# Loading q and k in 1 KB runs and turning them with smaller TensorE operations, in a sliding-window attention and channel-mix kernel

## The chip, the cores and the metric

The kernel runs on one core of a Trainium2 chip. The metric is the device time of one execution in microseconds (us), the median of the runs. With one core there are no dies to compare. The time before was 234.99 us, the median of 3 runs (234.88 to 235.05). Only runs in the fast state are compared. Their mean granted clock (the TensorE clock that the throttle let through, as a share of full speed) was 0.991 or more over a run.

## The reference

The first half is causal attention in a window of 128 positions with a distance bias per head. The second half is a channel mix with a shift by one position. Batch 8, 8 heads, 576 positions, 64 columns a head.

```python
def _attn_ref(q, k, v):                      # [8, 8, 576, 64], float32
    scores = scale * np.matmul(q, k.transpose(0, 1, 3, 2))
    rel = pos[:, None] - pos[None, :]
    bias = slopes[:, None, None] * (-np.abs(rel))[None, :, :]
    mask = (rel >= 0) & (rel < 128)
    scores = np.where(mask, scores + bias[None], -1e9)
    # ... softmax over the last axis ...
    return np.matmul(attn, v)

def _moe_ref(x, mu_k, mu_r, w_k, w_v, w_r):  # x [8, 576, 512], heads joined
    xk = mu_k * x + (1.0 - mu_k) * x_prev    # x_prev: one position earlier
    xr = mu_r * x + (1.0 - mu_r) * x_prev
    k = np.maximum(xk @ w_k, 0.0)            # 512 -> 1024
    v = k * k @ w_v                          # 1024 -> 512
    return sigmoid(xr @ w_r) * v             # the "receptance"
```

## The kernel before

The program is a list of operations with durations, dependencies and buffers. A list scheduler, run while the program is built, puts them in one fixed order for each engine. Each engine then works through its order and waits where data or a buffer is missing. So an edit of a duration or a priority moves instructions everywhere.

TensorE needs q and k turned, with the head's 64 columns on the partitions. They come in by several paths. The tails are the last 64 of the 576 positions.

```python
    WIDE = (1,)             # batches whose q and k are loaded head-major
    WAIT = 2.0              # how long 64-row operations may be put off
    QM = 0                  # 0: full transposes; 1: half-array ones
    XTT = range(6, B)       # batches whose tails a DMA turns
    NWARM = 90              # matmuls of a constant that keep TensorE busy early
    A = {PE: 14.25, ACT: 4.00, DVE: 4.50, VIR: 0}   # lead of attention over the mix
    NBIAS = 4               # head pairs that take the distance bias by matmul
    def SQ(order):          # engines allowed for the squares of the mix
        return (DVE,)
    # ...
    def run_load(dst, i, b, c0, r, h0, h1, deps=()):     # head-major: 64*r-value runs
        hs = (q, k)[i][b, h0:h1, c0:c0 + 128 * r].rearrange("h (p r) d -> p h (r d)", p=128)
        # ... one DMA on the software queue; r = 4 gives runs of 1 KB
    def full_load(b, i, h, g):                           # four loads in runs of 256 B
        src = (q, k)[i][b, :, 0:SM].rearrange("h (p r) d -> p h r d", p=128)
        # ...
    def tail_load(b):                                    # 64 partitions, runs of 256 B
        for i in range(2):
            src = (q, k)[i][b, :, SM:S].rearrange("h p d -> p h d")
            # ... dma_start(out=ts_buf[h.idx][64 * i:64 * i + 64], in_=src)
```

The transposes of a head pair, and the warm-up matmuls that the scheduler puts wherever its plan has TensorE idle:

```python
    for i in range(NWARM):      # lowest priority; no data, no result used
        plan.add(PE, 0.118 if i < 40 else 0.056, 0.0, [n_warm, g_wm], (1e12, i), emit_warm, ...)

    def qk_quad(b, g, nr, buf, ...):          # head-major: 32 transposes of 64x64
        for n in range(2 * nr):
            for hl, r in ((0, 0), (1, 1), (1, 0), (0, 1)):
                rows = slice(64 * r, 64 * r + 64)
                nc.tensor.transpose(
                    one(hp[r]).bitcast(BF16)[64 * hl:64 * hl + 64, 64 * n:64 * n + 64],
                    buf()[rows, n // nr, 2 * g + hl, n % nr], ident[rows, rows])
        # ... two copies of 512 columns to SBUF, on ScalarE after batch 0

    def qk_full(b, g, prio):                  # 8 transposes of 128x128
        for n in range(2 * NF):
            nc.tensor.transpose(..., cb_buf[hc.idx][:, n // NF, n % NF, 2 * g:2 * g + 2]..., ident)
        # ... one copy of 1024 columns on ScalarE

    def tails(b, prio):                       # 4 transposes of 128x128, one copy on VectorE
        for g in range(G):
            nc.tensor.transpose(..., ts_buf[hs.idx][:, 2 * g:2 * g + 2]..., ident)

    def square(e, out, in_):                  # k * k of the channel mix
        if e == ACT: nc.scalar.activation(out=out, in_=in_, func=AF.Square)
        else:        nc.vector.tensor_tensor(out=out, in0=in_, in1=in_, op=ALU.mult)
```

The softmax here doesn't subtract the row's maximum and nothing guards it: scores larger than these inputs give would overflow.

## Time and profile before

| | before |
|---|---|
| time, span of the profiled run | 234.99 us, 233.1 us |
| TensorE, VectorE, ScalarE busy | 97%, 81%, 69% |
| first receptance matmul (end of the start stage) | 37.38 us |
| last receptance group to the end of the span | TensorE dense, then a fixed end of 3.7 us |

The prediction below shows the page and the chain of waits. Here is the other view: the busy time of each engine in three stretches of 10 us. The columns are the stretch and its length, then for TensorE, its weight loads, VectorE, ScalarE and GpSimd the busy us with the number of instructions, and last the granted clock, the DMA share and GB/s.

```profile
30.00:40.00 10.00, 9.01 (x144) 6.54 (x144) 7.96 (x20) 9.47 (x19) 5.78 (x7) 1.00 1.59 181
40.00:50.00 10.00, 10.00 (x114) 5.34 (x113) 9.78 (x18) 5.85 (x9) 8.31 (x11) 1.00 2.14 176
50.00:60.00 10.00, 9.79 (x106) 6.26 (x105) 7.70 (x16) 9.30 (x17) 7.93 (x10) 1.00 2.27 186
```

### The profile page before, as it was taken

To read this page: it belongs to the slowest core of one execution; us is meant where nothing else is said; L and a number is where in the kernel's file an instruction comes from. 1 tells how busy PE (TensorE), PEld (TensorE's weight loads), DVE (VectorE), ACT (ScalarE), POOL (GpSimd) and SP (SyncE) were. 2 spreads that over 40 slices of the span, in tenths; PEclk is the share of its full clock that TensorE was granted. 3 is DMA by queue.
4 is the path that set the end of the run, shared out by engine and by line. 5 is a ranking of instruction groups with operands and counts; after the bars stand their busy time and mean duration, and the time that the engine had idled before them with its cause. 6 is when DMAs were issued, how large, how long until landed. Compare 5 with 4: busy or idle time off the path is not lost.

```text
span 233.1 us, 6268 instructions
## 1 busy us (share of the span) xinstructions
PE 225.8 (97%) x2487; PEld 135.7 (58%) x2487; DVE 189.8 (81%) x427; ACT 160.8 (69%) x292; POOL 97.7 (42%) x124
## 2 busy tenths in 40 slices
PE   7899989999999999999999999999999999999994
PEld 6576765556566765555555755455655844455462
DVE  7587988987797989989989979985769996974242
ACT  3669999759999986984984975947584726326251
POOL 8966773898883893069508935200000000000000
PEclk9999999999999999999999999999999999999999
DMA  7999999999999999989999999993232124121122
GB/s 168 178 167 196 161 162 185 153 199 201 155 154 173 109 138 207 106 106 169 201 188 100 172 181 211 155 146 106 69 89 93 45 48 146 46 90 48 65 70 90
DMA packets 131100, 31.73 MB, mean 136 GB/s; under 512 B 120056, under 2 KB 127232, under 8 KB 131072
## 3 DMA queue, kind: packets, MB, share of 16 engines
q0 software_dynamic: 102736, 16.26, 102.7%
q1 hardware_dynamic: 26592, 14.50, 26.9%
q10 hardware_dynamic: 1744, 0.59, 1.0%
q8 instruction: 19, 0.31, 0.5%
q14 instruction: 9, 0.07, 0.1%
HBM read 33.56 MB, written 9.44 MB: 184 GB/s over the span
## 4 chain that ended last, share of the span: by engine, by line
PE 84%; ACT 5%; DMA 3%; POOL 3%; issue 2%; DVE 1%; DVEq 0%; POOLq 0%; ACTq 0%
PE uno L941 27%; PE uno L907 26%; PE uno L925 14%; PE duo L716 6%; PE duo L658 5%; DMA ts<-in_k_dram 3%; PE uno L771 2%; PE uno L1154 2%; ACT at L672 2%; POOL qx L434 1%; ACT mask L1088 1%; ACT qk L628 1%; PE uno L856 1%; POOL vs L438 1%; ACT rl L914 1%
## 5 line engine op out<-in xcount | busy, mean ns | idle before, releaser
L941 PE MATMUL uno<-wv_sb,kk 128*128 128x512 bf16 (+2 forms) x296 | 71.8, 374 | 0.0
L907 PE MATMUL uno<-xk,wk_sb 128*128 128x256 bf16 (+2 forms) x416 | 69.5, 314 | 0.7 <-ACT rl L914 0.4
L672 ACT ACTIVATE at<-duo 128x1024 bf16<-128x1024 f32 (+2 forms) x68 | 65.7, 1002 | 5.4 <-PE duo L658 5.4
L914 ACT ACTIVATE rl<-uno 128x256 bf16<-128x256 f32 (+2 forms) x104 | 47.3, 492 | 20.3 <-PE uno L907 19.0
L907 PEld LDWEIGHTS <-wk_sb 128*128 128x128 bf16 x416 | 38.7, 98 | 22.1 <-issue 0.9
L685 DVE TENSOR_TENSOR at<-at,mask 128x1024 bf16<-128x1024 bf16 x56 | 37.7, 680 | 8.2 <-ACT at L672 7.8
L438 POOL DMA_DIRECT2D vs<-in_v_dram x32 | 28.4, 895 | 33.9 <-PE duo L716 30.3
L941 PEld LDWEIGHTS <-kk 128*128 128x128 bf16 x296 | 26.4, 98 | 26.2
L880 DVE TENSOR_TENSOR kk<-rl 128x256 bf16<-128x256 bf16 (+2 forms) x104 | 32.8, 334 | 9.0 <-ACT rl L914 7.8
L932 ACT ACTIVATE rs<-uno 128x512 bf16<-128x512 f32 x36 | 22.1, 614 | 26.1 <-PE uno L925 23.1
L925 PE MATMUL uno<-wr_sb,xr 128*128 128x512 bf16 x144 | 37.0, 379 | 0.5 <-ACT rl L914 0.5
L946 DVE SCALAR_TENSOR_TENSOR ot<-rs,uno 128x512 f32<-128x512 bf16 (+2 forms) x37 | 24.6, 668 | 12.1 <-PE uno L941 9.7
L716 PEld LDWEIGHTS <-at 128*128 128x128 bf16 x576 | 21.8, 98 | 6.0 <-issue 0.9
L821 DVE SCALAR_TENSOR_TENSOR xk<-dl,mu_sb,xt 128x576 bf16<-128x576 bf16 (+1 forms) x32 | 24.8, 780 | 0.4
L821 DVE SCALAR_TENSOR_TENSOR xr<-dl,mu_sb,xt 128x576 bf16<-128x576 bf16 (+1 forms) x32 | 24.4, 769 | 0.0
L463 POOL DMA_DIRECT2D cb<-in_k_dram x24 | 21.3, 901 | 7.1 <-DMA wv_sb<-in_moe_w_v_dram 3.3
L628 ACT COPY xt<-uno 128x256 bf16<-128x256 bf16 (+1 forms) x48 | 17.1, 405 | 9.0 <-PE uno L771 8.8
L925 PEld LDWEIGHTS <-xr 128*128 128x128 bf16 x144 | 13.5, 98 | 14.6 <-issue 0.7
L463 POOL DMA_DIRECT2D cb<-in_q_dram x24 | 21.2, 915 | 1.4 <-DMA vs<-in_v_dram 1.2
L628 ACT COPY qk<-uno 128x1024 bf16<-128x1024 bf16 (+2 forms) x26 | 18.8, 777 | 2.4 <-PE uno L1049 0.8
L716 PE MATMUL duo<-vs,at 128*128 128x65 bf16 x448 | 19.1, 193 | 0.0
L814 DVE TENSOR_TENSOR dl<-xt 128x576 bf16<-128x576 bf16 (+1 forms) x32 | 13.7, 434 | 4.2 <-ACT xt L628 4.2
(78 smaller groups left out, 206.8 us busy)
## 6 DMA issues: line engine op xcount, KB each, us to landing
out_dram<-ot SPq DMA_DIRECT2D x30, 256.0 KB, 5.2
vs<-in_v_dram POOLq DMA_DIRECT2D x32, 128.0 KB, 6.6
cb<-in_q_dram POOLq DMA_DIRECT2D x24, 128.0 KB, 7.0
cb<-in_k_dram POOLq DMA_DIRECT2D x24, 128.0 KB, 6.8
out_dram<-ot SPq DMA_DIRECT2D x10, 128.0 KB, 1.8
wk_sb<-in_moe_w_k_dram POOLq DMA_DIRECT2D x2, 512.0 KB, 8.8
wv_sb<-in_moe_w_v_dram POOLq DMA_DIRECT2D x2, 512.0 KB, 10.8
qx<-in_k_dram ACTq DMA_DIRECT2D x4, 128.0 KB, 4.5
```

Source lines behind the costliest of these rows:

```text
L438: return dma(POOL, 256, issue_t(1024), lambda e: nc.gpsimd.dma_start(out=vs_buf[h.idx][:, j, :, 0:D], in_=v[b, :, 128 * j:128 * j + 128].r ...
L463: return [dma(POOL, 256, issue_t(1024), lambda e, r=r: nc.gpsimd.dma_start(out=cb_buf[h.idx][:, i, r], in_=src[:, :, r]), [g]) for r in ra ...
L628: (nc.scalar.copy if e == ACT else nc.vector.tensor_copy)(out=out, in_=in_)
L672: lambda e, ah=ah, w=w, hp=hp: nc.scalar.activation(out=ah(), in_=two(hp)[:, :, 0:w], func=AF.Exp, scale=float(scale)), (), [hp])
L685: nc.vector.tensor_tensor(out=a, in0=a, in1=m, op=ALU.mult)
L716: nc.tensor.matmul(a[:, hl, t - t0], lhsT=at[:, lo:lo + 128], rhs=vs[:, u, 2 * g + hl, :] if u < NF else tvb[:, 2 * g + hl], start=(u == u ...
L821: lambda e: nc.vector.scalar_tensor_tensor(out=buf[hk.idx][:, g, e0 + c0:e0 + c1], in0=dls(), scalar=mu[:, g:g + 1], in1=xc(1), op0=ALU.mu ...
L880: nc.vector.tensor_tensor(out=out, in0=in_, in1=in_, op=ALU.mult)
L907: nc.tensor.matmul(one(hp)[:, 0:n], lhsT=wk_sb[:, po, 128 * fo:128 * fo + 128], rhs=xk_buf[hx.idx][:, po, c0:c1], start=(po == 0), stop=(p ...
L914: a = op(ACT, act_t(n), [s], pr, lambda e, hp=hp, hr=hr: nc.scalar.activation(out=rl_buf[hr.idx][:, 0:n], in_=one(hp)[:, 0:n], func=AF.Rel ...
L925: nc.tensor.matmul(one(hp), lhsT=xr_buf[hx.idx][:, po, 128 * c:128 * c + 128], rhs=wr_sb[:, po], start=(po == 0), stop=(po == NPO - 1))
L941: nc.tensor.matmul(one(hv)[:, a:b], lhsT=kk_buf[hk.idx][:, fo, o:o + 128], rhs=wv_sb[:, fo, a:b], start=(fo == 0), stop=(fo == NFO - 1))
```

## The change

The intent is to make q and k cheaper to bring in. Batches 2 and 3 are also loaded head-major in runs of 1 KB, and turned by 64x64 transposes, as batch 1 already was. The tails of batches 0 and 1 come as 1 KB runs over 128 partitions, and are turned by 16 matmuls with the identity instead of four transposes. Batch 4 goes from full to half-array transposes. The settings of the scheduler were searched again for it, so the order of all instructions differs. Squares of the first groups of the channel mix may also go to ScalarE.

```diff
-    WIDE = (1,)
+    WIDE = (1, 2, 3)
+    TW = (0, 1)
-    QUAD = 0.0565
+    QUAD = 0.040
-    WAIT = 2.0
-    QM = 0
+    WAIT = 5.0
+    QM = 1
     def SQ(order):
-        return (DVE,)
+        return (DVE, ACT) if order < 3 else (DVE,)
-    XTT = range(6, B)
+    XTT = range(5, B)
-    A = {PE: 14.25, ACT: 4.00, DVE: 4.50, VIR: 0}
-    NBIAS = 4
-    XRL = 3.0
+    A = {PE: 9.50, ACT: 6.00, DVE: 5.00, VIR: 0}
+    NBIAS = 5
+    XRL = 1.5
-    SLOPE = 4.5
+    SLOPE = 4.6
 # (the assumed DMA rates of run_load change too)
 # tail_load
+        if b in TW:
+            for i in range(2):
+                ns.append(dma(POOL, 104, issue_t(128), lambda e, i=i: nc.gpsimd.dma_start(
+                    out=ts_buf[h.idx].rearrange("p h d -> p (h d)")[:, 256 * i:256 * i + 256],
+                    in_=(q, k)[i][b, :, SM:S].rearrange("h (c r) d -> h c (r d)", r=4)), [g]))
+            return h, ns
 # tails, for b in TW
+            for n in range(8):
+                for hl in range(2):
+                    nc.tensor.matmul(
+                        one(hp)[64 * hl:64 * hl + 64, 64 * n:64 * n + 64],
+                        lhsT=ts_buf[hs.idx][:, n],
+                        rhs=ident.rearrange("p (g t c) -> p t g c", g=G, t=2)[:, hl],
+                        start=True, stop=True)
+        # two copies of 256 columns on VectorE in place of one of 512
 # (the old form stays as tails_full for the other batches; cut)
```

More of the change, by code (lines that the diff above doesn't have):

```diff
@@ L220 @@
     RATE = 284.0
-    WIDE = (1,)
+    WIDE = (1, 2, 3)
     PART_WIDE = True
-    QUAD = 0.0565
-    RUN = {2: 64 * 284 / 329.0, NF: 128 * 284 / 357.0}
+    TW = (0, 1)
+    QUAD = 0.040
+    RUN = {2: 64 * 284 / 345.0, NF: 128 * 284 / 390.0}
     FLIP = 1.25
     NO = 5
-    WAIT = 2.0
-    QM = 0
+    WAIT = 5.0
+    QM = 1
     OM = 1
@@ L843, in out_flip, with tails_full @@
         return res
-    def tails(b, prio):
-        htt = Hold("tt")
-        hs = th[b]
-        if b in XTT:
-            plan.follow(last["tt"], ttg[b])
-            last["tt"] = ttg[b]
-            return tth[b], ttl[b]
+    def tails_full(b, prio, htt, hs):
         hp = Hold("p1")
@@ L866, in tails, with emit @@
         c = [op(DVE, dve_t(512), [t, g], prio + (0,), emit_c, (), [hp])]
+        return htt, c
+    def tails(b, prio):
+        htt = Hold("tt")
+        hs = th[b]
+        if b in XTT:
+            plan.follow(last["tt"], ttg[b])
+            last["tt"] = ttg[b]
+            return tth[b], ttl[b]
+        if b not in TW:
+            return tails_full(b, prio, htt, hs)
+        hp = Hold("p1")
+        def emit(e):
+            for n in range(8):
[5 more added lines that the diff above has]
+                        start=True, stop=True)
+        t = op(PE, 0.03 * 16, list(tl[b]) + [n_ident], prio + (0,), emit, [hp], [hs])
+        g = virtual("tt", [htt])
+        c = [op(DVE, dve_t(256), [t, g], prio + (0,), lambda e, i=i: copy_any(
+            e, tt_buf[htt.idx][:, :, i].rearrange("p g (c r) -> p g c r", r=4),
+            one(hp)[:, 256 * i:256 * i + 256].rearrange("p (r g c) -> p g c r", r=4, g=G)),
+                (), [hp]) for i in range(2)]
         return htt, c
```

## The prediction

> **What bounds the kernel now.** I read the page first (busy shares, slices), then the chain of waits in order of time, then the timelines of TensorE and ScalarE over the first 60 us, and last the groups by form and the DMA queues by stretch.
>
> The page and the chain of waits:
>
> ```profile
> PE 225.8 (97%) x2487; PEld 135.7 (58%) x2487; DVE 189.8 (81%) x427; ACT 160.8 (69%) x292; POOL 97.7 (42%) x124
> ...
> PE 84%; ACT 5%; DMA 3%; POOL 3%; issue 2%; DVE 1%; DVEq 0%; POOLq 0%; ACTq 0%
> ```
>
> TensorE sets the end: 97% busy and 84% of the chain. But the busy share flatters it: before 26 us it holds 90 warm-up matmuls that compute nothing (L619), and the modelled tails of short matmuls cover gaps. So I split the span where the chain stops leaving TensorE.
>
> ```profile
> 8.60 8.04 DMA ts<-in_k_dram
> ...
> 18.08 1.30 ACT at L672 x2
> ...
> 25.84 1.56 PE uno L907 x12
> ...
> 37.38 1.02 PE uno L925 x4
> 38.41 0.55 PE duo L716 x18
> ...
> 44.43 0.55 PE duo L658 x12
> 44.98 0.97 PE uno L925 x4
> 45.95 0.86 PE uno L941 x4
> ...
> 53.23 1.02 ACT qk L628
> ...
> 85.47 0.42 ACT xt L628
> ...
> 227.23 2.18 PE uno L941 x12
> ```
>
> The reader is to see three stages. Up to 37.4 us the chain goes through a tail load of batch 0 (8 us) and then mostly through ScalarE; this is the only stage with slack. From 37.38 to 229.4 us it is TensorE alone but for two waits, 1.08 us at 53.2 and 0.46 us at 85.5. From 229.4 on there is a fixed end of 3.7 us (last eviction, store).
>
> The same chain gives prices. Four 512-column matmuls take 0.86 us (0.2155 each), 0.97 right after a group that used 64 rows of the array: a change of tiling costs about 0.11. Twelve score matmuls take 0.55, of which 0.11 is the change before them.
>
> The timeline of TensorE:
>
> ```profile
> 16.69 0.40 PE L856 MATMUL uno<-ident,ts 128*128 128x128 bf16 x4
> ...
> 32.35 0.45 PE L1002 MATMUL uno<-ident,cb 64*64 64x64 bf16 x32
> 32.73 1.05 PE L907 MATMUL uno<-xk,wk_sb 128*128 128x256 bf16 x8
> ...
> 52.58 1.50 PE L1154 MATMUL uno<-ident,cb 128*128 128x128 bf16 x24
> ```
>
> The start of the next group is what counts: 32 quarter-array transposes (one head pair of batch 1) occupy 32.35 to 32.73, 0.38 with the change of tiling, so 0.28 without. Eight full transposes (one head pair of batches 2 to 4) take 0.45 (16 of them are 0.89 or 0.90 in the chain). Ten half-array transposes (L771) take 0.25 with the change, 0.14 without.
>
> **What the Trainium skill says.** (1) "Trainium Kernel Development and Optimization", Performance Expectations: matmul busy time is a bad measure because matmuls are pipelined. The trace agrees: 97% busy, yet only about 25 us of useful matmul work lies in the first 37.4 us (below). (2) "TensorE: Matmul & The Clock Gate", Back-to-back issue gap: N / 2.4 GHz plus 2.5 ns; for 512 columns 216 ns, and the trace has 0.86 us for four. (3) "TensorEngine Tiling (Array Packing)", Key Properties: changing the tiling mode drains TensorE. The trace shows the price, 0.97 against 0.86. (4) "DMA: Bandwidth & Descriptors", Why small descriptors are slow: a fixed overhead per packet weighs heavily at 256 B. In the queue view for 17 to 24 us (mostly the 1 KB runs of batch 1) the software queue moved 1.32 MB in 7 us, 0.189 MB/us; for 62 to 70 us (256 B runs of a later batch) 1.05 MB in 8 us, 0.131 MB/us. It agrees.
>
> **The change, part by part.** Instruction counts are from the order of the built programs, prices from above.
>
> TensorE, whole program:
> - Batches 2 and 3, eight head pairs, from 8 full transposes to 32 quarter ones: 8 x (0.28 - 0.45) = -1.4 us.
> - Batch 4, four pairs, from 8 full to 16 half ones: 16 x 0.0145 = 0.23, so 4 x (0.23 - 0.45) = -0.9 us.
> - Tails of batch 5 move to the transposing DMA: -0.2 us.
> - Tails of batches 0 and 1: four full transposes (0.22) become 16 matmuls with K = 128 and 64 output rows, 64 columns each. At an issue floor of 25 to 30 ns each that is 0.4 to 0.5: 2 x +0.2 = +0.4 us. (If both column halves overlapped it would be nil.)
> - One more head pair (batch 1, first) takes its bias by matmul: 4 more of 512 columns, +0.9 us.
> - Changes of tiling shape: I counted them in both orders, with (rows, columns) as the shape: 106 before, 120 after; 14 x 0.11 = +1.5 us. The quarter transposes have a shape of their own, so they pay on both sides.
> Sum: -1.4 - 0.9 - 0.2 + 0.4 + 0.9 + 1.5 = +0.3 us. The new transposes win nothing on TensorE that the drains do not take back.
>
> Check of this bookkeeping: with these prices all matmuls from the first receptance matmul (37.38 us) to the last sum to about 191 us; the trace has 229.4 - 37.4 = 192.0, of which 1.5 are the two named waits. So that stage is dense, and only removed work or removed waits shorten it.
>
> The two waits: at 52.6 us four head pairs of full transposes are issued in a row, take all four single-bank PSUM buffers, and each is freed only by a 1.04 us copy on ScalarE. After the change the order interleaves 32 quarter transposes with score and channel-mix groups, and the copies are two of about 0.6 us. I give back 0.8 of the 1.5 us.
>
> The start: tails of batch 0 as 128 runs of 1 KB instead of 512 of 256 B per tensor. Two loads of 64 KB at 0.131 MB/us are 1.0 us of queue, at 0.189 0.7 us: they land 0.3 to 0.6 us earlier. ScalarE then works nearly without a gap (9.72 of 10 us in 20 to 30, 9.47 in 30 to 40), so what is gained there holds only if ScalarE gets no more work before the first receptance matmul. I summed its instructions up to the first receptance activation at columns / 1200 plus 0.07 us (0.10 for squares and masks): 28.0 us before, 28.2 after. Fewer relus stand ahead of it (10 instead of 16), but six squares are new there. So about even, and the first receptance matmul needs slightly less of it. TensorE has about 1 us less to do before that point (24 against 25 us), which it then does later. Net for the start: first receptance matmul 0.8 us earlier, but 1 us more left behind it, which is already in the sum.
>
> So from the first receptance matmul on: before 190.5 dense + 1.5 waits; after 190.5 + 0.3 + 1.0 (moved behind) = 191.8 + 0.7 waits = 192.5. End: 37.4 - 0.8 + 192.5 + 3.7 = 232.8 against 233.1.
>
> DMA in the middle: q and k of each of batches 2 and 3 are 1.05 MB as written, 5.5 us of queue at 0.189 MB/us instead of 8 at 0.131. This lies under a TensorE that is already full: worth nothing directly, though buffers and orders get easier.
>
> VectorE and ScalarE: 13 squares go from VectorE (13 x 0.25 = 3.3 us) to ScalarE (about 13 x 0.33 = 4.3), two mask products (1.4 us) vanish, and twelve copies of 1.04 become 24 of about 0.55. VectorE was at 9.8 of 10 us in 40 to 50, 90 to 100 and 110 to 120, so relief there can remove small stalls; ScalarE between 38 and 60 us, where it was at 5.9 to 9.3 of 10, becomes nearly full. I count -0.5 for the first (and the retuned priorities, which were presumably searched for this order) and +0.2 for the second.
>
> Sum: -0.3 - 0.3 = -0.6, and I lean a little further, to -0.9: 234.1 us.
>
> **Rivals.**
> (a) DMA-bound start. If the loads, not ScalarE, pace the first 37 us, the 1 KB runs give more: the 8.04 us tail load stands on the chain, and the POOL timeline shows issues waiting for older DMAs (2.13 us for a weight load at 13.5). Against it: after 17.4 us ScalarE has a single gap of 0.25 us. If it holds the start shrinks by 2 to 3 us: 232.
> (b) ScalarE takes over. Squares and doubled copies sit on the engine that bounds the start and nearly fill it to 60 us. My sums give ScalarE 19.7 us and TensorE about 21.5 us of work between the first receptance activation and the first 384-column relu; with such a balance any slip stalls TensorE. It would make 236 or 237.
> (c) Drains dearer than thought. If quarter transposes and the 128x64 tail matmuls pay 0.2 a change, 14 more changes make +1.3 us over my sum: 235.5.
> (d) Hidden anyway. TensorE is full from 37 us on, everything else cancels: 235.
>
> **Range and chances.** The terms are small and of both signs; (a) and (b) set the ends. Predicted 234.1 us, 8 in 10 within 231.9 to 236.2. A gain over 2% needs 230.3 or less, 4.7 us off a start that has about 12 us of slack, most of it unavoidable loading: 0.06. A loss over 2% needs 239.7: 0.03. Within 2%: 0.91.
>
> **What would show it.** TensorE's instructions rise by about 250. The tail load of batch 0 lands before 16.3 us, and the first receptance matmul starts at 36.2 to 37. The wait at 53 us is gone or below 0.5 us. A quarter group of 32 occupies 0.28 to 0.4 us, the 16 tail matmuls 0.4 to 0.5. ScalarE is over 9 of 10 us in 40 to 60; packets under 512 B fall by about 18,400 from 120,056 (2 x 8192 of q and k, 2 x 1024 of tails). I am wrong if the first receptance matmul comes 2 us earlier or later than that, if TensorE shows waits for ScalarE between 40 and 60 us, or if the stretch behind it is not 191 to 194 us.

## More of the kernel before

The timeline of TensorE shows two waits at the transposes of the tails of batch 1:

```profile
29.53 0.27 PE L856 MATMUL uno<-ident,ts 128*128 128x128 bf16 x2 [0.17 <-ACT qk L628]
30.29 0.27 PE L856 MATMUL uno<-ident,ts 128*128 128x128 bf16 x2 [0.49 <-issue]
```

They are not waits for the load: both tails of batch 1 had landed by 28.48 us. The second is put down to "issue", that is, to nothing that the profile shows.

## The result, and the profile after

| | before | after |
|---|---|---|
| time, median of 4 runs each | 235.02 us (234.88 to 235.27) | 236.23 us (235.61 to 236.46) |
| span of the profiled run | 233.1 us | 234.4 us |
| VectorE, ScalarE busy | 81%, 69% | 80%, 71% |
| first receptance matmul | 37.38 us | 36.78 us |

The ratio is 1.0046, with a 95% interval of 1.0025 to 1.0067. Here and below, a ratio is the mean time of one kernel's fast runs over the mean of the other's fast runs of the same rounds, so it is not quite the ratio of the medians. The change is the same within 2%, and slower by about 1.1 us. I had expected 0.9 us faster.

The page of the changed kernel, in the lines for busy time, DMA packets and the chain by engine:

```profile
PE 223.1 (95%) x2703; PEld 134.7 (57%) x2735; DVE 186.8 (80%) x413; ACT 165.8 (71%) x317; POOL 89.4 (38%) x116
...
DMA packets 118062, 31.90 MB, mean 136 GB/s; under 512 B 102536, under 2 KB 114064, under 8 KB 118032
...
PE 83%; ACT 9%; DMA 2%; issue 2%; DVE 1%; SPq 1%; DVEq 0%
```

The trace lacks 32 matmul records: there are 2735 weight loads and 2703 matmuls. So the busy 223.1 us is not less work. ScalarE rises from 5% to 9% of the chain. The same three stretches show where:

```profile
30.00:40.00 10.00, 7.79 (x155) 5.21 (x156) 6.18 (x15) 9.26 (x19) 4.52 (x7) 1.00 1.36 197
40.00:50.00 10.00, 9.48 (x184) 6.61 (x184) 8.97 (x16) 9.53 (x21) 6.91 (x9) 1.00 1.84 183
50.00:60.00 10.00, 9.74 (x195) 5.72 (x195) 9.39 (x19) 9.46 (x18) 7.80 (x10) 1.00 2.00 187
```

In 40 to 50 us ScalarE went from 5.85 to 9.53 us, and TensorE from 10.00 to 9.48. The chain of waits after, in that stretch, leaves TensorE for almost 9 us:

```profile
39.57 0.88 PE uno L954 x4
...
40.96 1.02 ACT at L679
41.98 0.59 ACT xt L635 x2
...
44.90 1.85 ACT at L679 x2
46.75 0.29 ACT kk L907
...
49.23 0.48 ACT qk L635
```

The pieces on ScalarE are exponentials (at), copies of turned values (xt, qk) and squares (kk), which were never on ScalarE before. In the kernel before, the chain in the same stretch is TensorE alone.

**A ledger.** TensorE is nearly dense, so I sorted its span into work and idle time. Work is the number of instructions of each kind times a price from the trace of before: 0.2155 us for 512 columns, 0.0145 for a half-array transpose, 0.0088 for a quarter one, 0.105 for each change of tiling shape, and so on; the new tail matmuls, which are only in the trace of after, at 0.0175. Idle is the start of a receptance group less the work ahead of it. The prices can be checked where TensorE is dense: from the fifth to the seventh receptance group of after (66 to 75 us) there are 9 changes of shape, 4 of them to or from the quarter transposes, and the idle time stays at 14.3 within 0.02 us. One correction is needed. The last of the four early loads of q lands at a slightly different time in each execution. This shows as the wait for it in the timeline of TensorE, here before, and then after:

```profile
7.65 1.06 PE L1046 MATMUL uno<-id,qx 128*128 128x128 f32 x7 [0.54 <-DMA qx<-in_q_dram]
```

```profile
7.97 1.05 PE L1075 MATMUL uno<-id,qx 128*128 128x128 f32 x7 [0.85 <-DMA qx<-in_q_dram]
```

The instructions up to this point are the same in both. So I take the start of the first group of bias matmuls behind the first attention group (9.57 us before, 9.89 after) as the arrival, and subtract its delay against 9.57 from all starts of a trace. In the 12 experiments it lies between 9.63 and 10.73 us. The correction is my choice. It assumes that all later work moves along, and that is not so for a wait for another load.

| us on TensorE, corrected for the arrival | before | after | difference |
|---|---|---|---|
| work ahead of the first receptance matmul | 24.57 | 23.15 | -1.42 |
| idle ahead of it | 12.81 | 13.31 | +0.50 |
| work behind it | 191.12 | 192.53 | +1.41 |
| idle from it to the third receptance group (at 45 and 50 us) | 0.01 | 0.72 | +0.71 |
| idle from there to the fifth (at 61 and 66 us) | 0.39 | 0.29 | -0.10 |
| idle from there to the last group | 0.77 | 0.59 | -0.18 |
| sum | | | +0.92 |

The corrected spans differ by 0.99 us (233.06 and 234.05), the times by 1.1. So the loss sorts itself like this: TensorE has as much work as before (-0.01 us), and 0.93 us more idle time. Of that 0.50 lies ahead of the first receptance matmul, and 0.71 between 37 and 50 us; 0.28 is won back later.

### The profile page after: what moved, and what is told of

Its sections match the earlier page's. It is cut to its first block, busy times and chain, and to the rows that moved or that the text cites. A ratio compares the mean times of both kernels' runs of the same rounds, so it can differ in the third digit from the quotient of the medians.

```text
span 234.4 us, 6737 instructions
## 1 busy us (share of the span) xinstructions
PE 223.1 (95%) x2703; PEld 134.7 (57%) x2735; DVE 186.8 (80%) x413; ACT 165.8 (71%) x317; POOL 89.4 (38%) x116
## 4 chain that ended last, share of the span: by engine, by line
PE 83%; ACT 9%; DMA 2%; issue 2%; DVE 1%; SPq 1%; DVEq 0%
PE uno L970 26%; PE uno L936 24%; PE uno L954 13%; PE duo L723 6%; PE duo L665 6%; ACT at L679 4%; DMA qx<-in_q_dram 2%; PE uno L778 2%; ACT qk L635 2%; PE uno L1031 1%; PE uno L626 1%; PE duo L652 1%; ACT rl L943 1%; ACT kk L907 1%; PE uno L723 1%
## 5 line engine op out<-in xcount | busy, mean ns | idle before, releaser
L970 PE MATMUL uno<-wv_sb,kk 128*128 128x512 bf16 (+2 forms) x280 | 69.5, 373 | 1.6 <-issue 1.1
L692 DVE TENSOR_TENSOR at<-at,mask 128x1024 bf16<-128x1024 bf16 x54 | 36.0, 676 | 6.5 <-ACT at L679 6.4
L909 DVE TENSOR_TENSOR kk<-rl 128x256 bf16<-128x256 bf16 (+2 forms) x91 | 29.8, 343 | 11.2 <-ACT rl L943 9.8
L954 PE MATMUL uno<-wr_sb,xr 128*128 128x512 bf16 x133 | 36.3, 379 | 1.2 <-ACT qk L635 0.7
L635 ACT COPY qk<-uno 128x512 bf16<-128x512 bf16 (+1 forms) x38 | 20.5, 599 | 2.4 <-PE uno L1031 1.0
L734 DVE TENSOR_TENSOR xu<-duo,rc 128x640 bf16<-128x640 f32 x20 | 16.4, 818 | 0.3
L470 POOL DMA_DIRECT2D cb<-in_k_dram x16 | 14.3, 914 | 1.3 <-DMA vs<-in_v_dram 0.8
```

The lines of the kernel that those rows point to most:

```text
L635: (nc.scalar.copy if e == ACT else nc.vector.tensor_copy)(out=out, in_=in_)
L692: nc.vector.tensor_tensor(out=a, in0=a, in1=m, op=ALU.mult)
L954: nc.tensor.matmul(one(hp), lhsT=xr_buf[hx.idx][:, po, 128 * c:128 * c + 128], rhs=wr_sb[:, po], start=(po == 0), stop=(po == NPO - 1))
L970: nc.tensor.matmul(one(hv)[:, a:b], lhsT=kk_buf[hk.idx][:, fo, o:o + 128], rhs=wv_sb[:, fo, a:b], start=(fo == 0), stop=(fo == NFO - 1))
```

## The experiments

Unless I say that the plan was made anew, an edit is made when instructions are emitted, after the scheduler has fixed the order. Then the order of all engines stays that of the kernel it starts from, and only the named instructions differ. All kernels gave correct results. The ledger of all of them:

| run | ratio to before, 95% | work | idle, first receptance | idle, third | idle, last |
|---|---|---|---|---|---|
| before | 1 | 215.69 | 12.81 | 12.82 | 13.98 |
| after | 1.0046 (1.0025 to 1.0067) | 215.68 | 13.31 | 14.03 | 14.91 |
| e1_sq_dve | 1.0045 (1.0028 to 1.0062) | 215.68 | 13.75 | 14.13 | 15.34 |
| e2_old_tails | 1.0040 (1.0021 to 1.0059) | 215.14 | 14.36 | 15.09 | 15.85 |
| e3_full | 1.0188 (1.0153 to 1.0223) | 215.78 | 13.31 | 18.61 | 19.38 |
| e4_sq_dve_replanned | 1.0251 (1.0224 to 1.0277) | 215.37 | 12.22 | 13.01 | 20.60 |
| e5_fewer_warm | 1.0011 (0.9994 to 1.0029) | 215.68 | 13.02 | 13.74 | 14.49 |
| e7_copies_dve | 1.0029 (1.0006 to 1.0052) | 215.68 | 12.82 | 13.97 | 14.73 |
| e8_before_copies_dve | 1.0038 (1.0021 to 1.0055) | 215.69 | 13.14 | 14.01 | 15.18 |
| e9_before_fewer_warm | 0.9993 (0.9972 to 1.0013) | 215.69 | 13.04 | 13.05 | 14.21 |
| e10_both | 1.0031 (1.0009 to 1.0052) | 215.68 | 12.54 | 13.89 | 14.65 |
| e11_late_sq_dve | 1.0044 (1.0000 to 1.0089) | 215.68 | 13.03 | 13.41 | 14.97 |
| n2_search | 1.0075 (1.0046 to 1.0104) | 214.46 | 11.47 | 11.48 | 16.29 |
| n2_fw | 1.0050 (1.0010 to 1.0090) | 214.36 | 12.97 | 12.98 | 16.56 |

Work and idle time are in us, summed up to the start of the first, third and last receptance group, and corrected for the arrival. n2 has another order, so its groups stand elsewhere. They come from one trace each, the ratios from 4 to 6 runs. Where the two disagree by a few tenths, I trust neither alone.

**Are the squares on ScalarE the cost?** e1_sq_dve, from the changed kernel:

```diff
-                e, kk_buf[hk.idx][:, fo, 0:n], rl_buf[hr.idx][:, 0:n]), (), [hr]))
+                DVE, kk_buf[hk.idx][:, fo, 0:n], rl_buf[hr.idx][:, 0:n]), (), [hr]))
```

> The changed kernel in its own order, with the 13 squares that its schedule gave to ScalarE run on VectorE instead; nothing else moves. Theory A (ScalarE, loaded with squares and doubled copies, stalls TensorE between 37 and 54 us, where the idle grew by about 0.7 us): 235.3 to 235.7 us, the waits of TensorE for ScalarE between 40 and 50 us shrink. Theory B (the loss is the 14 extra changes of tiling shape and the added bias): nothing moves, 236.2. VectorE has room there (6.2 of 10 us in 30 to 40), so a loss is not expected of either.

Measured: 236.46 us (236.19 to 236.72), no gain. The theory that the squares cost the difference falls as a whole, but the ledger shows why it looked right. From the first to the third group the idle time falls from 0.72 to 0.38 us: there ScalarE was too full, and moving the squares takes away about half of the wait. It is only a net gain, because the chain of e1 runs through VectorE in that stretch, from 43.2 to 48.6 us, where that of the changed kernel runs through ScalarE:

```profile
43.63 0.60 DVE at L692
...
48.37 0.21 DVE kk L909
```

The start takes this gain back, with 0.44 us more idle time ahead of the first receptance matmul. The timeline of VectorE in e1, in a part of the start where it works almost without a gap:

```profile
28.27 0.28 DVE L909 TENSOR_TENSOR kk<-rl 128x256 bf16<-128x256 bf16 x1
28.47 0.55 DVE L734 TENSOR_TENSOR xu<-uno,rc 128x384 bf16<-128x384 f32 x1
```

Squares now stand ahead of the attention outputs (xu), which TensorE needs next. In the changed kernel the same xu starts at 27.84 us instead of 28.47, with the same arrival of 9.89 us.

e4_sq_dve_replanned asks for the same, but lets the scheduler plan anew:

```diff
-        return (DVE, ACT) if order < 3 else (DVE,)
+        return (DVE,)
```

> The same choice as in the first run (squares on VectorE only), but given to the scheduler, which then lays out the whole kernel anew with the changed kernel's other settings. Theory A alone would say 235.3 to 235.7 as in the first run. Theory D (the scheduler's layout scatters by some microseconds with any setting, and both kernels are picks from that scatter): clearly slower, 238 to 241 us, with idle of TensorE in other places.

Measured: 241.35 us (240.53 to 242.01). The work is even 0.31 us less, and the idle time 5.7 us more, nearly all of it behind the third group. About 1.7 us of that is clock: the trace has a granted clock of 0.5 from 61.17 us on, for 3.41 us. Still, a new plan with one choice changed moved the time by some 5 us, far more than the edit is worth in place. That is why the other experiments keep the order, and why the separate effect of the changed settings (A, WAIT, XRL, SLOPE) could not be measured.

e11_late_sq_dve, the last run, starts from e5_fewer_warm below and moves only the squares after the first group, which run from about 37 us on (eight of the 13 by the trace, not seven):

```diff
-                e, kk_buf[hk.idx][:, fo, 0:n], rl_buf[hr.idx][:, 0:n]), (), [hr]))
+                DVE if order else e, kk_buf[hk.idx][:, fo, 0:n], rl_buf[hr.idx][:, 0:n]), (), [hr]))
```

> The changed kernel in its own order with the first 68 warm-up matmuls only (that version: 235.81 us, ratio 1.0011), and on top only the squares of the second and later channel-mix groups (7 of the 13, those after 36 us) moved from ScalarE to VectorE in place. Theory H, each stretch has its own engine at the limit: at 24 to 28 us VectorE is the full one and ScalarE squares are right, at 37 to 50 us ScalarE is the full one and VectorE has gaps of 0.2 to 0.65 us, so these squares are better on VectorE: the idle before the third receptance group falls by 0.3 to 0.4 us, 235.4 to 235.5 us, level with the kernel before. Rival I, the rest of the idle there is set by copies and exponentials that stay on ScalarE: no change, 235.7 to 235.9. Over 236 would mean VectorE is full there as well.

Measured: 237.09 us (236.43 to 237.39), where before ran from 234.71 to 237.34 on this chip. In time it is a miss, with a wide interval (1.0000 to 1.0089). Over 236 us had been the sign that VectorE is full there as well, and the chain agrees: from 43.3 to 48.7 us it runs through VectorE, as in e1. The ledger tells more. Against e5 the start is unchanged (13.03 and 13.02), the idle time from the first to the third group falls from 0.72 to 0.38, as in e1, and then it rises by 1.12 us between the fifth and the eighth group (66 to 86 us), where e5 has 0.28. Uncorrected, this trace starts a full us late: it waited 1.33 us for that load of q, against 0.54 and 0.85 in the two lines above, after a wait of 0.41 that they do not have.

So two traces agree that moving the squares between 37 and 50 us takes 0.34 us off this wait, net of what they cost on VectorE. They also agree that the later squares (three, at 61.8 to 65.8 us) are no better there: from the fifth to the eighth group e1 takes 0.48 us longer than the changed kernel, and e11 0.84 us longer than e5.

**What are the new tails worth?** e2_old_tails keeps the changed order, with the old tail loads and transposes for batches 0 and 1:

```diff
-                    out=ts_buf[h.idx].rearrange("p h d -> p (h d)")[:, 256 * i:256 * i + 256],
-                    in_=(q, k)[i][b, :, SM:S].rearrange("h (c r) d -> h c (r d)", r=4)), [g]))
+                    out=ts_buf[h.idx][64 * i:64 * i + 64],
+                    in_=(q, k)[i][b, :, SM:S].rearrange("h p d -> p h d")), [g]))
-            for n in range(8):
-                for hl in range(2):
-                    nc.tensor.matmul(...)
+            for g in range(G):
+                nc.tensor.transpose(..., ts_buf[hs.idx][:, 2 * g:2 * g + 2]..., ident)
```

> The changed kernel in its own order, with the tails of batches 0 and 1 loaded and turned in the old way (512 runs of 256 B per tensor, four full transposes each) in the same places. Bookkeeping of TensorE work: 0.9 us less (no 128x64 shape, four changes of shape fewer, 0.22 instead of 0.48 us each). Theory B (work and drains decide): 235.3 to 235.8 us. Rival C (the start is bound by the loads): the tail lands about 0.5 us or more later, and the time rises to 236.7 or more. If both are true they cancel: 236.2.

Measured: 236.28 us (235.9 to 236.97): the parts cancel. The old form needs 0.54 us less work, because 32 matmuls become 8 transposes and four changes of shape go away. But the idle time ahead of the first receptance matmul rises by 1.05 us. The tails of batch 1 are late for this order, whose plan counted on them:

```profile
28.65 0.38 PE L883 MATMUL uno<-ident,ts 128*128 128x128 bf16 x4 [0.97 <-ACT kk L904]
```

The line names ScalarE, but the k tails of batch 1 landed at 28.52 us, just before. In the changed kernel they landed at 27.18, and this group starts at 28.11 without a wait. So the new tails are worth 0.5 us at the first receptance matmul (1.05 less 0.54). At the end it is 0.4 by the ledger and nothing by the times.

**What are the head-major loads worth?** e3_full keeps the changed order, but loads batches 2 and 3 in runs of 256 B and turns them by full transposes:

```diff
 # run_load, for b in (2, 3): four loads in place of the two halves
+            nc.gpsimd.dma_start(out=cb_buf[ch[b].idx][:, i, a], in_=(q, k)[i][b, :, a:SM:4].rearrange("h p d -> p h d"))
+            for a in range(4) if h0 == 0
 # qk_quad, for b in (2, 3): 8 transposes of 128x128 in place of 32
+                for n in range(2 * nr):
+                    nc.tensor.transpose(..., cb_buf[ch[b].idx][:, n // nr, n % nr, 2 * g:2 * g + 2]..., ident)
```

> The changed kernel in its own order, with q and k of batches 2 and 3 loaded in 256 B runs (8 loads a batch as before) and turned by 64 full transposes in place of 256 quarter ones, same copies. Bookkeeping of TensorE work: +0.1 us (0.45 instead of 0.28 us each, but fewer changes of shape). Theory B: 236.1 to 236.4 us, quarter transposes and head-major loads are worth nothing. Rival C (loads matter): the 16,384 packets of 256 B that come back slow the loads of 30 to 60 us and TensorE shows waits for batch 2; 237 us or more.

Measured: 240.05 us (238.52 to 241.16), 3.8 us slower than the changed kernel (3.3 by the ratios). The work is the same within 0.1 us: dearer transposes against 12 fewer changes of shape. Most of the time goes to the load. These are TensorE's waits (in total us, times, longest us) and then the chain:

```profile
PE uno L1032 <- DMA cb<-in_k_dram: 2.5, 4, 0.7
```

```profile
40.65 6.46 DMA cb<-in_k_dram
...
47.16 0.23 PE uno L1032
```

The first eight transposes of batch 2 take from 43.28 to 47.32 us, where 0.45 would do: 3.6 us for the load. Right behind it the granted clock halves, from 47.37 us on for 3.41 us. This is one microsecond of that stretch (the clock is the third figure from the end):

```profile
49.00:50.00 1.00, 1.00 (x4) 0.34 (x3) 0.00 (x0) 1.00 (x2) 0.98 (x2) 0.50 2.31 147
```

Four matmuls of 512 columns take 1.68 us there in place of 0.86. Half clock for 3.41 us is another 1.7 us, by my estimate. The two make up the 5.3 us of idle time between the first and the third group. The times agree: the three runs with a mean clock of 0.993 or less took 240.64 to 241.16 us, the other three 238.52 to 239.46.

The loads in runs of 256 B end at 47.1 us. The changed order wants batch 2 at 43.3, where the kernel before turned it only at 51.04. The head-major loads come in halves of four heads: in the changed kernel the first half had landed at 42.70 us and the second at 45.31. So the first heads are there 4.4 us earlier than in e3, but the whole batch only 1.8. Part of the gain is thus the split by heads and not the 1 KB runs, and no run separates the two. The runs are faster all the same: loads of batch 3 land one after another at 0.193 MB/us (as written) in the changed kernel and at 0.136 in e3, those of batch 2 at 0.171 and 0.155. But before had no wait for that load at all. The earliness is needed only by the order that was built on it, and TensorE is full at that time.

**Warm-up matmuls in the way.** The changed trace has fillers around the first tails:

```profile
16.18 0.83 PE L626 MATMUL uno<-warm 128*128 128x128 bf16 x12
16.94 0.44 PE L884 MATMUL uno<-ident,ts 128*64 128x64 bf16 x16
...
18.27 0.68 PE L626 MATMUL uno<-warm 128*128 128x128 bf16 x9
18.78 0.60 PE L936 MATMUL uno<-xk,wk_sb 128*128 128x256 bf16 x4
```

They were planned into gaps that the plan expected. They have a fixed place in TensorE's order, so work behind them can't start when its data comes early. e5_fewer_warm, from the changed kernel, and e9_before_fewer_warm, the same in the kernel before as a control, emit only the first 68 of the 90:

```diff
+        n_done.append(0)
+        if len(n_done) > 68:
+            return
         nc.tensor.matmul(one(h_wm)[:, 0:128], lhsT=warm, rhs=warm, start=True, stop=True)
```

> The changed kernel in its own order, without the last 22 of its 90 warm-up matmuls, among them nine that stand for 0.5 us right before the first channel-mix group at 18.3 us. Theory E (TensorE itself loses there, because these fillers stand in its order): 0.5 us or so faster, 235.7. Theory F (ScalarE and VectorE bound the start, TensorE's place there is slack): no change, 236.0 to 236.5, the first receptance matmul at the same time.

> The control to the run without late fillers: the kernel before in its own order, without the last 22 of its 90 warm-up matmuls. Dropping them was worth about 0.8 us to the changed kernel. In the kernel before they stand ahead of the tail of batch 0, which lands only after them (16.65 us), and at 22.6 and 23.7 us. Theory E (the fillers hide the earlier tail of the changed kernel and so are part of why the change lost): 0 to 0.3 us here, 235.1 to 235.5. Rival G (fillers cost both kernels alike): about 0.8 us faster here too, 234.7, and they explain nothing of the difference.

Measured: e5 235.81 us (235.49 to 236.21), e9 235.31 (234.63 to 235.59). Ratios of 1.0011 and 0.9993: without the fillers the changed kernel is some 0.8 us faster by the ratios (0.4 by the medians and by the ledger), and in the kernel before nothing can be seen. This is not firm. The intervals of the changed kernel and of e5 overlap, and two later runs with the same fillers left out and one more edit each, e10 and e11, stand at 1.0031 and 1.0044. The timelines fit it. In e5 the tails and the first mix now wait only for a VectorE copy:

```profile
16.43 0.44 PE L887 MATMUL uno<-ident,ts 128*64 128x64 bf16 x16 [0.24 <-DVE qk L638]
...
18.17 0.60 PE L939 MATMUL uno<-xk,wk_sb 128*128 128x256 bf16 x4 [0.35 <-DVE tt L638]
```

In e9 TensorE waits for the tail load itself. It lands at 17.35 us in this trace, and landed at 16.64 in that of before, where the fillers ended at the same moment (16.69):

```profile
17.39 0.40 PE L859 MATMUL uno<-ident,ts 128*128 128x128 bf16 x4 [1.07 <-DMA ts<-in_k_dram]
```

So in the traces a part of what the new tail loads give was hidden behind fillers.

**Copies in the start.** From 31 to 37 us the chain of the changed kernel is ScalarE alone:

```profile
31.62 1.83 ACT at L679 x2
33.45 0.96 ACT qk L635 x2
34.41 1.84 ACT at L679 x2
36.25 0.48 ACT qk L635
```

Meanwhile VectorE waited 2.95 us at one place (for an exponential, up to 35.37). e7_copies_dve moves the four qk copies of the last two head pairs of batch 1 to it; e8_before_copies_dve does so in the kernel before:

```diff
-            e, qk_buf[hq.idx][:, :, c0 + w * r:c0 + w * r + w]...
+            DVE if b == 1 and g > 1 else e, qk_buf[hq.idx][:, :, c0 + w * r:c0 + w * r + w]...
```

> The changed kernel in its own order, with the four key/query copies of batch 1, head pairs 2 and 3, which stand on ScalarE at 33.3 to 37.2 us between the exponentials, run on VectorE, which waits 2.95 us there. Theory F (ScalarE sets the start in 30 to 37 us; the tails that now land in time only move the wait onto it): the first receptance matmul about 1 to 1.4 us earlier, at 35.4 to 35.8 us, and the time 235.0 to 235.4. Theory B (total work of TensorE): nothing, 236.2.

> The kernel before in its own order, with the same four copies on VectorE. They stand there at 29.9 to 31 us and at 34.6 and 37.7 us, and VectorE is fuller (8.0 of 10 us in 30 to 40, with squares to do). Theory F: less to gain than in the changed kernel, 0 to 0.8 us: 234.3 to 235.1. If it gains as much as the changed kernel does (1 us or more), then the copies tell nothing about why the change lost.

Measured: e7 236.03 us (235.96 to 237.54), e8 236.44 (236.22 to 236.97). e7 gains 0.49 us of idle time at the first receptance matmul, and gives 0.43 back at the second, because the attention output on VectorE now queues behind the copies:

```profile
36.08 1.02 PE L954 MATMUL uno<-wr_sb,xr 128*128 128x512 bf16 x3 [0.86 <-DVE qk L635]
38.01 0.32 PE L778 MATMUL uno<-ident,xu 64*128 64x64 bf16 x10 [0.37 <-DVE xu L734]
```

e8 is a miss: I had expected up to 0.8 us of gain, and it lost 1. VectorE has no room there in the kernel before (its idle time rises by 0.33 us at the first and 1.19 at the third group).

e10_both joins e5 and e7:

> The changed kernel in its own order with both repairs: without the last 22 fillers, and with the four copies of batch 1 on VectorE. If the two gains (0.8 and about 0.4 us) stand in different places and add up: 235.0, level with the kernel before or just under it. If both shorten the same wait: 235.7, as the better one alone.

Measured: 236.0 us (235.8 to 236.66), no better than e5 alone. The two do add up at the first receptance matmul: its idle time is 12.54, the lowest of all with this order, and 0.77 below the changed kernel (0.29 from e5 and 0.49 from e7 make 0.78). Then 0.43 is lost at the second group, and 0.92 instead of 0.72 on the way to the third. A start that ends earlier only runs sooner into the stretch in which ScalarE and VectorE set the pace.

**A search for a version that beats both.** n2_search lets the scheduler plan with the measured price of every change of shape (by rows and columns, 0.105 us) and of the tail matmuls, and searches the settings again:

```diff
-                        if n.rows[0] != rows:
+                        if (n.rows[0], n.cols) != (rows, cols):
                             n.dur = dur = dur + self.SWITCH
-    WIDE = (1, 2, 3)
-    TW = (0, 1)
-    QUAD = 0.040
+    WIDE = (1, 2)
+    TW = (0,)
+    QUAD = 0.035
+    TAIL = 0.40
-    A = {PE: 9.50, ACT: 6.00, DVE: 5.00, VIR: 0}
+    A = {PE: 35.75, ACT: 4.5, DVE: 0.0, VIR: 0}
```

(WAIT, XRL, SLOPE, AHEAD, XD, XTT, NBIAS, the squares and the copies of batches 1 and 2 changed with it.)

> A kernel laid out anew: its scheduler counts a change of tiling in columns too (quarter transposes and the 64-column tail matmuls), may give the copies of batches 1 and 2 to VectorE, and its settings were searched. It keeps the new tail loads for batch 0 only and head-major q and k for batches 1 and 2. TensorE work by my bookkeeping: 214.7 us, against 215.7 (before) and 216.1 (changed). Theory H (what counts is TensorE work plus the idle of the first 54 us): with the idle of the kernel before (14.0 us) 234.0, with that of the changed one 234.9. If the idle comes out larger, the scheduler's picture of the waits is off, and the time is 236 or more.

Measured: 237.0 us (236.16 to 240.69). n2_fw, the same with 68 warm-up matmuls:

> The searched kernel in its own order, without the last 22 fillers. As in the changed kernel they stand between 14 and 26 us in front of work that may be ready: 0.3 to 0.8 us faster than the searched kernel with them.

Measured: 236.29 us (235.64 to 240.55). Each ran slow in one of six executions. The medians and ranges here hold it, the ratios leave it out. That n2_fw has 1.5 us more idle time ahead of the first group than n2_search is a matter of its trace: it has one wait of 2.0 us at 30.4 us that the profile puts down to nothing. The search found what it was told to find: 1.2 us less work than the changed kernel, and in n2_search the shortest idle time ahead of the first receptance matmul (11.47). It loses more than that to waits later, with an idle time of 16.29 and 16.56 at the last group. So the scheduler's picture of work is good and its picture of waits is not. No version that I ran beats the kernel before; e5 and e9 are level with it.

## Why the prediction was right or wrong

**Right in size, wrong in sign: the time.** It moved by less than 2%, as predicted, but up by 1.1 us and not down by 0.9; at 236.23 us it lies 0.03 above the upper end of the range. (The ratio of 1.0046 on the 234.99 us that the prediction started from gives 236.07.) That it came so near is in part luck, since errors of both signs cancel, as shown below.

**Right: the work on TensorE.** I predicted +0.3 us from new transposes, drains, tails and the bias; the ledger has -0.01. The single prices hold but for the tails. A quarter group of 32 takes 0.38 us with its change of shape, from 25.39 to 25.77:

```profile
25.39 0.45 PE L1031 MATMUL uno<-ident,cb 64*64 64x64 bf16 x32
25.77 0.61 PE L936 MATMUL uno<-xk,wk_sb 128*128 128x256 bf16 x4
```

The 16 tail matmuls take 0.38 us (16.94 to 17.32, with the change of shape behind them), so 0.28 without it, where I had 0.4 to 0.5. The single records of the trace show why: the matmuls start in pairs, 3 to 4 ns apart, and each pair 28 to 29 ns after the last. So the two column halves do overlap, which the prediction had only in brackets. (The second group, 28.11 to 28.61, keeps the same pace. Its other 0.12 us come before the matmul that follows.) That is the 0.3 us by which my sum was too high. Weight loads rise by 248 (2735 against 2487), against about 250. Packets under 512 B fall by 17,520, against 18,400. No run measured a transpose or a change of shape by itself.

**Nearly right: the start.** I predicted the first receptance matmul 0.8 us earlier with 1 us less work ahead of it, so 0.2 more idle. It is 0.6 earlier (36.78), or 0.92 corrected for the arrival, with 1.42 less work and 0.50 more idle. Of that idle time 0.29 are the fillers (e5), which I had not seen. The tail load of batch 0 landed 0.3 us earlier (16.34 against 16.64), at the low end of the 0.3 to 0.6 foreseen and just after the 16.3 that was named as a sign. Rival (a), a start bound by loads that gains 2 to 3 us, fails: late tails do cost 1.05 us of idle time in the changed order (e2), but the new ones gave 0.5 us there, since ScalarE is the chain from 31 to 37 us and fillers stood in the way.

**Wrong: "I give back 0.8 of the 1.5 us", -0.5 for VectorE and the retuned priorities, and the lean of -0.3.** The wait at 53 us did go, as predicted, and from the third group on the idle time falls by 0.28 us. But a new one of 0.7 us arose between 37 and 50 us, where the kernel before had none. So idle time behind the first receptance matmul rose by 0.43 us, where I had it fall by 0.8 for the waits and by 0.3 net for the engines. With the lean of 0.3, that makes 1.8 us, nearly all of the error of 2.0 (1.1 and 0.9). The errors of the start (+0.3 idle) and of the work (-0.3) cancel.

**Wrong: the size of ScalarE's part.** The prediction lists "+0.2 for the second", a nearly full ScalarE, and names TensorE waiting for ScalarE between 40 and 60 us as a sign of being wrong. That sign is there: it is rival (b), which named 236 or 237, though 0.50 us of the new idle time lies in the start. I saw that ScalarE would be full (over 9 of 10 us predicted, 9.53 and 9.46 found), and priced it at 0.2. The idle time of TensorE in that stretch is 0.7. Moving the squares takes 0.34 off it, shown twice in the ledger (e1, e11). The other 0.38 stands with VectorE as the chain, so it does not tell what is left on ScalarE. In the changed kernel the earlier copies of batch 2 are there too, since its transposes moved from 51.04 to 43.3 us, and they may be the rest. No run tested that alone.

**Rival (c), dearer drains, and (d), hidden anyway.** (c) fails: with 0.2 for a change to or from the quarter transposes, the idle time from 66 to 75 us would have come out 0.4 us lower at the end than at the start, and it stayed level. (d) is half of the truth: the faster transfers are real (e3), and hidden.

**What stays open.** The runs do not show how much each retuned setting contributes, since a new plan moved the time by more than the effect (e4), nor how much the fillers cost in time. They do not separate the part of e3's load time that is due to the runs of 1 KB from the part that is due to the split by heads. And the ledger's tenths rest on one trace a kernel.

## What to carry to other kernels

When one engine is full, an earlier load or a cheaper transpose on it is worth only the work that it takes off that engine; count the changes of tiling shape on both sides of each small operation before believing in it. Look at what the earliness pulls forward: here the new plan put copies and squares into a stretch where ScalarE had been the engine with most room, and used that room up (9.53 of 10 us, from 5.85). And correct single traces for chance at their start (here up to 1.2 us) before reading tenths of a us out of them; fillers placed by a plan should be tested by leaving them out. Look at the granted clock of the stretch too, not only at its mean over the run: half clock for 3.41 us was 1.7 us of what looked like idle time in e3 and e4.

## What the Trainium skill lacked or had wrong

- "TensorEngine Tiling (Array Packing)", Key Properties, says that a change of tiling mode drains TensorE and gives no price. Here each change costs about 0.105 us (0.97 against 0.86 us for four matmuls, and an idle time that stays level over 9 changes), and with 120 of them (106 before) that is 12.6 us of the span.
- "TensorE: Matmul & The Clock Gate", Part 4: PE-mode transpose, gives about 275 ns for a 128x128 transpose within a kernel. That can't be used as a price in a row of them: here 8 take 0.45 us, 56 ns each, and 32 quarter-array ones 0.28 us without the drain, under 9 ns each.
- No page that I read says how much the arrival of the early loads varies between executions, with the instructions up to there the same. Here the first work behind them started at 9.57 to 10.73 us, up to 1.16 us later than in the profile of before.
